# A transfer window of 1.5 MB, a seed product over 128 partitions, and the w_spatial sums on VectorE

## The chip, the core and the metric

The kernel runs on one core of a Trainium2 chip. The core has TensorE (PE; its weight loads are listed apart as PEld), VectorE (DVE), ScalarE (ACT), GpSimd (POOL), and SyncE (SP), which here issues nearly all transfers. Sixteen DMA engines move the data. The metric is the device time of one execution in microseconds. Everything is in 32-bit floats; a product on TensorE is made of three passes over operands that are split into a high part and a remainder (float32r).

## The reference

Chunked attention, then a gated MLP with a product over the positions. There are 4 batches, 8 heads of 64, 768 positions, chunks of 32 with 16 positions of context on the left and 8 on the right, and 8 memory positions.

```python
for c in range(nc):                      # 24 chunks of 32 positions
    k_full = concat([mem_k, k[l_start:r_end]]); v_full = concat([mem_v, v[l_start:r_end]])
    a = softmax(scale * q_c @ k_full.T)
    out[c] = a @ v_full
x = heads joined                         # (4, 768, 512)
h = maximum(x @ w_in, 0)                 # w_in (512, 1024)
u, v = h[..., :512], h[..., 512:]
v_n = (v - mean(v)) / sqrt(var(v) + 1e-6)
v_s = einsum('ts,bsd->btd', w_spatial, v_n) + b_spatial[None, :, None]
out = (u * v_s) @ w_out
```

w_in and w_out come as 64-bit floats and are turned into 32-bit ones on the chip.

## The kernel before

The kernel does not write its instructions in the order in which they run. Every piece of work is entered into a planner (`Plan`, lines 26 to 129) with its engine, an estimated duration, what it reads and writes, and a rank. `Plan.order` (64) simulates the engines and the transfers: at each step it takes, over all engines, the piece that can begin first, and among those of one engine the one with the lowest rank. `Plan.emit` (127) then issues all pieces in that order. The order on each engine, SP included, is thus fixed when the kernel is built. For transfers the planner assumes 0.30 MB per us for all of them together, 2 us for the landing, and that a transfer is not issued before the eighth transfer ahead of it has landed (lines 88 and 89). Loads that are entered with `seq=True` keep the order in which they are entered.

The work itself has two stages.

*Attention and first products.* 24 units of 128 positions (`attend`, 479): 64 small products for the scores of unit i and 64 for the weighted values of unit i - 1 (`burst`, 361, all on line 364), softmax on VectorE and ScalarE, transposes (448, 463). Behind each half of a batch come the products with w_in (`group`, 489, lines 501 to 503, 12 matmuls each). Their results are stored to DRAM: the normalized v by `ffn_v` (store on line 558, 256 KB) and u by `ffn_u` (store on line 575, 192 KB, from the ring `uo` of two buffers). The loads at the start are entered in this order (lines 921 to 936): the memory keys and values on ScalarE's queue; then on SP q and k of the first unit, two parts of w_in, v of unit 0 in four pieces, two parts of w_in, q and k of the second unit, v of unit 1, q and k of the next two units, v of unit 2, and the four parts of w_in for u.

*The products with w_spatial and w_out* (`product`, 609). Both are computed for each batch by a scheme of seven block products, p1 to p7, over quarters of the operands, in place of eight. Four sums of quarters, s1 to s4, are built on the left side: `total` (615, instruction on line 623) takes 128x768 elements at a time on the engine named by `sum_eng`, which is "POOL" in `spatial` (690, given on line 736) and "DVE" in `ffn_o` (739, given on line 782). `left` (627) splits each operand into a high part on ScalarE (636) and a remainder on VectorE (639). `blocks` (644) issues the matmuls (661). For w_spatial, the first product into a sum bank is preceded by a seed (655): a matmul of `ones` and `bias`, which adds b_spatial. Both have 64 partitions: row 0 holds the high part of the bias, row 32 its remainder, and all others are zero (`load_bias`, 893). There are 16 seeds, 4 in each batch. The results are copied from the banks (703, 752), joined (709, 758), and for w_spatial multiplied by u on POOL (717); for w_out they are stored (764). Of each batch, the first step for w_spatial is entered ahead of all steps for w_out of the batch before, and the other six behind them.

Of the kernel before, what the change touches and what calls it, by code (L numbers as in the profile page):

```python
# [9 lines left out]
F32R = mybir.dt.float32r  # L10
# [15 lines left out]
class Plan:  # L26
# [7 lines left out]

    def __init__(self, rings, loose, rate, landing, lat):
        self.rings, self.loose = rings, loose
        self.rate, self.landing, self.lat = rate, landing, lat
        self.ops, self.writer, self.readers, self.slots, self.newest = [], {}, {}, {}, {}
# [25 lines left out]
    def order(self):  # L64
# [17 lines left out]
        while len(out) < len(ops):  # L82
            best = None
            for e, ns in waiting.items():
                pick = None
                for n in ns:
                    t = max(free[e], ready[n], free["POOL"] if ops[n][9] else 0.0, lone if e == "POOL" else 0.0)
                    if ops[n][5] and len(landed) >= 8:
                        t = max(t, landed[-8])
                    for s in ops[n][7]:  # L90
                        have = taken[s[0]]
                        if s not in have and len(have) >= self.rings[s[0]]:
                            old = self.slots[have[-self.rings[s[0]]]]
                            t = max([t] + [end.get(m, 1e9) for m in old])
                    if t >= 1e9:
                        continue
                    late = max(t, free[e])
                    c = (late, ops[n][4], n)
                    if pick is None or c < pick:
                        pick = c  # L100
                if pick and (best is None or pick < best[0]):
                    best = (pick, e)
# [9 lines left out]
            if mb:  # L112
                pipe = max(pipe, t + us) + mb / self.rate
                end[n] = pipe + self.landing
                landed.append(end[n])
            else:
                end[n] = t + us + tail
            self.start[n] = t
            out.append((t, n))
            for m in users[n]:  # L120
                left[m] -= 1
                if not left[m]:
                    ready[m] = max([end[d] + self.lat for d in ops[m][3]] + [self.start[d] for d in ops[m][8]])
                    waiting[ops[m][0]].append(m)
        return [n for _, n in sorted(out)]

    def emit(self):
# [5 lines left out]
def tile_chunked_attention_gmlp(  # L133
# [45 lines left out]
             "q": 2, "k": 2, "kT": 2, "p": 1, "xs": 1, "pT": 1, "vr": 2, "op": 4, "sm": 2, "ug": 6, "ot": 8}  # L179
    plan = Plan(sizes, {"f", "y", "st", "big", "ot"}, rate=0.30, landing=2.0, lat=0.06)  # L180
    op = plan.op
# [20 lines left out]
    wsp = const.tile([P, 7, 2, HU, HT], F32R, name="wsp")  # L202
    bias = const.tile([D, 2, HT], F32R, name="bias")
    ones = const.tile([D, P], F32R, name="ones")
    ident = const.tile([P, P], F32, name="ident")
# [31 lines left out]
    line = {}  # L237

    def load(dst, src_, w, rank, r=(), eng="SP", slow=1.0, us=0.45, seq=False):
        e = {"SP": nc.sync, "ACT": nc.scalar, "POOL": nc.gpsimd}[eng]  # L240
        n = 4
        for s in src_.shape:
            n *= s
        mb = n / 1e6 * slow
        n = op(eng, us, lambda: e.dma_start(out=dst() if callable(dst) else dst, in_=src_), r=r, w=w, rank=rank, mb=mb,  # L245
               after=line.get(eng) if seq else None)
        if seq:
            line[eng] = n
# [273 lines left out]
    def ffn_v(b, tt):  # L522
# [26 lines left out]
        def norm():  # L549
# [7 lines left out]
        op("DVE", 0.43, norm, r=[("rstd", i)], w=[k_], rank=rank, alone=True)  # L557
        op("SP", 0.45, lambda: nc.sync.dma_start(out=vn_far[i // HU][:, i % HU], in_=t_["st", s]), r=[k_],
           w=[("vn_far", i // HU, i % HU)], rank=rank, mb=P * DH * 4e-6)

    def ffn_u(b, hf, d):
# [4 lines left out]
        def pair(c):  # L566
# [7 lines left out]
        far_ = u_far[(b * 2 + d // 2) * 2 + hf][:, d % 2]  # L574
        op("SP", 0.45, lambda: nc.sync.dma_start(out=far_, in_=t_["uo", i]), r=[("uo", i)],
           w=[("u_far", (b, d // 2, hf), d % 2)], rank=rank, mb=P * HT * 4e-6)
# [113 lines left out]
    def spatial(b):  # L690
# [4 lines left out]
        def done(name, p, bank):  # L695
# [37 lines left out]
            elif name == "p3":  # L733
                join("u2", bank)
                gate("u2", 0, 1)
        return product("s", b, ["p1", "p2", "p6", "p5", "p7", "p4", "p3"], [quarter(0, 0), quarter(0, 1), quarter(1, 0), quarter(1, 1)], HU, 2 * P, 2, HT,
                lambda i, x, s: wsp[:, i, x, s], lambda i: [("wsp", s, i) for s in range(HU)], "POOL", True, done)

    def ffn_o(b):
# [4 lines left out]
        def done(name, p, bank):  # L744
# [16 lines left out]
            def store(x, th, nh):  # L761
                r0 = (1 - th) * HT + p * P
                to = out[b, r0:r0 + P, nh * HN:(nh + 1) * HN]
                op("SP", 0.45, lambda: nc.sync.dma_start(out=to, in_=t_[ot(x)]), r=[ot(x)], rank=rank, mb=HN * P * 4e-6)
            if name == "p1":
# [127 lines left out]
    def load_bias(rank):  # L893
# [3 lines left out]
        def clear():  # L897
            t_[raw] = alloc("big", "bias", [P, 1024], U32).bitcast(F32)
            nc.gpsimd.memset(t_[raw][0:D], 0.0)
            nc.gpsimd.memset(t_[raw][0:D, S:S + P], 1.0)  # L900
        op("POOL", 0.8, clear, r=[("wsp", 2, 6)], w=[raw], rank=rank)
# [4 lines left out]
        def relative():  # L906
            a = t_[raw][0:D, HT:S]
            nc.gpsimd.tensor_tensor(a, a, t_[raw][0:D, 0:HT], op=ALU.subtract)

        def high():  # L910
            nc.scalar.copy(bias.rearrange("p h n -> p (h n)"), t_[raw][0:D, 0:S])
            nc.scalar.copy(ones, t_[raw][0:D, S:S + P])

# [111 lines left out]
```

## Time and profile before

| | us |
|---|---|
| median of 3 runs | 416.65 |
| range of the runs | 415.87 to 418.09 |
| the profiled execution | 417.55 |
| its span in the trace | 415.8 |
| busy in the span: PE, PEld | 375.4, 334.2 |
| busy in the span: DVE, ACT, POOL | 270.7, 192.8, 177.6 |
| mean granted TensorE clock | 0.979 |

The profile covers one execution. Matmuls overlap, so the distance between starts tells more than a duration. "PEclk" or the granted clock is the share of full speed that TensorE was given. The DMA share is the mean busy share of the 16 engines; it can be a little over 1, since packets overlap. In a timeline or a group, the bracket or the last column tells how long the engine had been idle and what ended that; "issue" is idle time in which the engine waited for nothing that the profile shows. "SPq" is the issuing of transfers by SP.

### The profile page before, as it was taken

How to read it: one execution, taken by the hardware profiler on the slowest of the kernel's cores; microseconds unless marked ns; L12 is line 12 of the kernel's file. 1: busy time of each engine (PE TensorE's matmuls, PEld its weight loads, DVE VectorE, ACT ScalarE, POOL GpSimd, SP SyncE). 2: the span in 40 equal slices, each digit the busy share in tenths (PEclk: the TensorE clock that was granted, in tenths of full speed). 3: DMA queues.
4: the chain of work that ended last, by engine and by line, in shares of the span. 5: the costliest groups of instructions: out<-in, count | busy, mean ns of one | idle time of the engine just before them, and what ended most of it. 6: DMA issues, size and time to landing. Idle time of an engine off the chain costs nothing.

```text
span 415.8 us, 11823 instructions
## 1 busy us (share of the span) xinstructions
PE 375.4 (90%) x4972; PEld 334.2 (80%) x4972; DVE 270.7 (65%) x446; ACT 192.8 (46%) x344; POOL 177.6 (43%) x167
## 2 busy tenths in 40 slices
PE   1576888799899799899999999999999999999985
PEld 0354667689798698788888899998999899989985
DVE  3656858385496596747686467668736883697373
ACT  3645426354554355434553347336434533552271
POOL 5322336553474095601131189443633364336510
PEclk9996689999999999999999999999999999999999
DMA  8999519828676766555732638306421542231004
GB/s 209 254 287 202 184 48 273 254 72 273 181 223 189 202 221 170 161 180 172 249 126 96 210 125 292 115 0 210 166 83 38 202 143 74 74 104 52 0 2 152
DMA packets 47369, 65.13 MB, mean 157 GB/s; under 512 B 4434, under 2 KB 38866, under 8 KB 47316
## 3 DMA queue, kind: packets, MB, share of 16 engines
q1 hardware_dynamic: 46900, 64.25, 51.0%
q8 instruction: 39, 0.64, 0.6%
q10 hardware_dynamic: 416, 0.13, 0.1%
q14 instruction: 14, 0.11, 0.1%
HBM read 45.49 MB, written 18.87 MB: 155 GB/s over the span
## 4 chain that ended last, share of the span: by engine, by line
PE 74%; DMA 10%; DVE 6%; issue 6%; ACT 2%; SPq 1%; ACTq 0%; DVEq 0%
PE y L661 17%; PE f L661 13%; PE f L501 11%; PE f L503 10%; PE f L502 10%; PE sx L364 8%; DMA vmain<-in_v_dram 6%; DVE op L639 3%; PE xt L463 2%; PE pt L448 2%; DMA k<-in_k_dram 2%; ACT op L636 1%; SPq L245 1%; DMA big<-in_moe_w_out_dram 1%; DVE ot L758 1%
## 5 line engine op out<-in xcount | busy, mean ns | idle before, releaser
L717 POOL TENSOR_TENSOR ug<-st,ug 128x384 f32<-128x384 f32 x32 | 41.6, 1310 | 30.5 <-DVE st L709 28.2
L661 PE MATMUL y<-wsp,op 128*128 128x384 f32 x288 | 54.0, 341 | 0.0
L661 PEld LDWEIGHTS y<-wsp,op 128*128 128x128 f32 x288 | 50.2, 188 | 1.5 <-issue 1.5
L501 PE MATMUL f<-x,win_h 128*128 128x384 f32 x128 | 46.2, 361 | 0.0
L636 ACT CAST op<-sm 128x768 fp32r<-128x768 f32 x32 | 26.7, 837 | 40.7 <-POOL sm L623 15.0
L639 DVE TENSOR_TENSOR op<-sm,op 128x768 fp32r<-128x768 f32 x32 | 34.2, 1068 | 15.9 <-ACT op L636 15.9
L503 PE MATMUL f<-x,win_h 128*128 128x384 f32 x128 | 43.2, 337 | 0.0
L501 PE MATMUL f<-win_h,x 128*128 128x512 f32 x96 | 43.1, 449 | 0.0
L502 PE MATMUL f<-x,win_l 128*128 128x384 f32 x128 | 43.0, 336 | 0.0
L547 POOL TENSOR_TENSOR rstd<-ve,mhalf 128x1 f32<-128x1 f32 x24 | 15.3, 638 | 64.3 <-DVE ve L543 64.0
L661 PE MATMUL f<-wsp,op 128*128 128x384 f32 x216 | 41.4, 342 | 0.0
L502 PE MATMUL f<-win_h,x 128*128 128x512 f32 x96 | 39.6, 413 | 1.3 <-issue 1.3
L503 PE MATMUL f<-win_l,x 128*128 128x512 f32 x96 | 39.6, 413 | 0.4 <-issue 0.4
L661 PEld LDWEIGHTS f<-wsp,op 128*128 128x128 f32 x216 | 37.4, 188 | 1.5 <-issue 1.1
L661 PE MATMUL y<-wout,op 128*128 128x256 f32 x288 | 36.3, 280 | 1.4 <-DVE op L639 0.9
L661 PEld LDWEIGHTS y<-wout,op 128*128 128x128 f32 x288 | 34.9, 188 | 2.0 <-DVE op L639 1.3
L400 DVE TENSOR_TENSOR xs<-sx,rec 128x512 f32<-128x512 f32 x24 | 16.5, 688 | 29.1 <-PE sx L364 29.1
L364 PE MATMUL sx<-vmain,pT 64*32 64x64 f32 x1536 | 24.5, 228 | 9.9 <-issue 8.9
L364 PEld LDWEIGHTS sx<-kmain,q 64*32 64x32 f32 x1536 | 17.9, 112 | 18.6 <-issue 10.1
L364 PE MATMUL sx<-kmain,q 64*32 64x64 f32 x1536 | 22.4, 238 | 10.7 <-ACT kmain L350 7.5
L364 PEld LDWEIGHTS sx<-vmain,pT 64*32 64x32 f32 x1536 | 20.2, 107 | 12.9 <-issue 11.0
L661 PE MATMUL f<-wout,op 128*128 128x256 f32 x216 | 28.1, 282 | 2.5 <-DVE st L758 2.3
(91 smaller groups left out, 766.0 us busy)
## 6 DMA issues: line engine op xcount, KB each, us to landing
vmain<-in_v_dram SPq DMA_DIRECT2D x48, 128.0 KB
vn_far<-st SPq DMA_DIRECT2D x24, 256.0 KB
u_far<-uo SPq DMA_DIRECT2D x32, 192.0 KB
vr<-vn_far SPq DMA_DIRECT2D x8, 768.0 KB
ug<-u_far SPq DMA_DIRECT2D x16, 384.0 KB
q<-in_q_dram SPq DMA_DIRECT2D x11, 512.0 KB
out_dram<-ot SPq DMA_DIRECT2D x36, 128.0 KB
vmain<-in_v_dram SPq DMA_DIRECT2D x47, 96.0 KB
```

The costliest lines, as they stand in the source:

```text
L364: nc.tensor.matmul(o, w_, m, start=True, stop=True, skip_group_check=True)
L400: nc.vector.tensor_tensor(xs.rearrange("p t r d -> p r t d"), t_["sx", i][:, :, 1], rec.rearrange("p t r -> p r t").unsqueeze(3).broadcast ...
L448: nc.tensor.transpose(a[:, t], p[:, t], ident)
L463: nc.tensor.transpose(a[:, t], xs[:, t], ident)
L501: nc.tensor.matmul(o, lh, rh, start=(j == 0), stop=False)
L502: nc.tensor.matmul(o, ll, rh, start=False, stop=False)
L503: nc.tensor.matmul(o, lh, rl, start=False, stop=(j == len(pairs) - 1))
L547: nc.gpsimd.tensor_tensor(a, t_["ve", i], mhalf, op=ALU.pow)
L636: nc.scalar.copy(half(0), of())
L639: nc.vector.tensor_tensor(half(1), of(), half(0).bitcast(F32), op=ALU.subtract)
L661: nc.tensor.matmul(o, x, y, start=first and m == 1 and not (seed and bank != "x"), stop=m == 3 * chunks, skip_group_check=True)
L717: nc.gpsimd.tensor_tensor(g, t_[st(x)], g, op=ALU.mult)
```

## The change

Three parts. A list `flight` takes down every transfer in the order of emission with its size in MB (the planner's own number: loads of q and k count 1.15 times, loads of v 1.2 times). Before a transfer is issued, `held_by` goes back through that list and adds up sizes, the new one included; the transfer at which the sum passes 1.5 MB, or else the eighth one back, must have landed first. The planner uses the same rule for its estimates, in place of the eighth one alone. Second, `bias` and `ones` have 128 partitions, and the clearing, the difference and the copies that make them cover 128 partitions; the added rows are zero in `bias`. Third, the four sums of `spatial` go to VectorE, in the planner (whose price for VectorE is 0.17 + 0.00102 us per element of a row, for POOL 0.15 + 0.0024) as in the code.

```diff
-    def __init__(self, rings, loose, rate, landing, lat):
+    def __init__(self, rings, loose, rate, landing, lat, window):
...
-                    if ops[n][5] and len(landed) >= 8:
-                        t = max(t, landed[-8])
+                    if ops[n][5]:
+                        t = max(t, self.held_by(landed, ops[n][5], 0))
...
-                landed.append(end[n])
+                landed.append((end[n], mb))
...
+    def held_by(self, flight, mb, none):
+
+        for back, (name, size) in enumerate(reversed(flight), 1):
+            mb += size
+            if back == 8 or mb > self.window:
+                return name
+        return none
...
-    plan = Plan(sizes, {"f", "y", "st", "big", "ot"}, rate=0.30, landing=2.0, lat=0.06)
+    plan = Plan(sizes, {"f", "y", "st", "big", "ot"}, rate=0.30, landing=2.0, lat=0.06, window=1.5)
...
-    bias = const.tile([D, 2, HT], F32R, name="bias")
-    ones = const.tile([D, P], F32R, name="ones")
+    bias = const.tile([P, 2, HT], F32R, name="bias")
+    ones = const.tile([P, P], F32R, name="ones")
...
+    flight = []
+
+    def transfer(e, out_, in_, mb):
+        ins = e.dma_start(out=out_, in_=in_)
+        wait = plan.held_by(flight, mb, None)
+        if wait:
+            tc.add_manual_dep(ins.ins, wait, mybir.DependencyInfo(mybir.DependencyClass.Sync, mybir.DependencyReason.DATA),
+                              reason="pace")
+        flight.append((ins.ins.name, mb))
...
-        n = op(eng, us, lambda: e.dma_start(out=dst() if callable(dst) else dst, in_=src_), r=r, w=w, rank=rank, mb=mb,
+        n = op(eng, us, lambda: transfer(e, dst() if callable(dst) else dst, src_, mb), r=r, w=w, rank=rank, mb=mb,
...
-                lambda i, x, s: wsp[:, i, x, s], lambda i: [("wsp", s, i) for s in range(HU)], "POOL", True, done)
+                lambda i, x, s: wsp[:, i, x, s], lambda i: [("wsp", s, i) for s in range(HU)], "DVE", True, done)
...
-            nc.gpsimd.memset(t_[raw][0:D], 0.0)
-            nc.gpsimd.memset(t_[raw][0:D, S:S + P], 1.0)
+            nc.gpsimd.memset(t_[raw][0:P], 0.0)
+            nc.gpsimd.memset(t_[raw][0:P, S:S + P], 1.0)
...
-            nc.scalar.copy(bias.rearrange("p h n -> p (h n)"), t_[raw][0:D, 0:S])
-            nc.scalar.copy(ones, t_[raw][0:D, S:S + P])
+            nc.scalar.copy(bias.rearrange("p h n -> p (h n)"), t_[raw][0:P, 0:S])
+            nc.scalar.copy(ones, t_[raw][0:P, S:S + P])
```

The stores on lines 558, 575 and 764 go through `transfer` in the same way, and the difference on line 908 covers 128 partitions.

More of the change, by code (lines that the diff above doesn't have):

```diff
@@ L26 @@
 class Plan:
-    def __init__(self, rings, loose, rate, landing, lat):
+    def __init__(self, rings, loose, rate, landing, lat, window):
         self.rings, self.loose = rings, loose
-        self.rate, self.landing, self.lat = rate, landing, lat
+        self.rate, self.landing, self.lat, self.window = rate, landing, lat, window
         self.ops, self.writer, self.readers, self.slots, self.newest = [], {}, {}, {}, {}
@@ L557, in ffn_v @@
         op("DVE", 0.43, norm, r=[("rstd", i)], w=[k_], rank=rank, alone=True)
-        op("SP", 0.45, lambda: nc.sync.dma_start(out=vn_far[i // HU][:, i % HU], in_=t_["st", s]), r=[k_],
+        op("SP", 0.45, lambda: transfer(nc.sync, vn_far[i // HU][:, i % HU], t_["st", s], P * DH * 4e-6), r=[k_],
            w=[("vn_far", i // HU, i % HU)], rank=rank, mb=P * DH * 4e-6)
@@ L574, in ffn_u @@
         far_ = u_far[(b * 2 + d // 2) * 2 + hf][:, d % 2]
-        op("SP", 0.45, lambda: nc.sync.dma_start(out=far_, in_=t_["uo", i]), r=[("uo", i)],
+        op("SP", 0.45, lambda: transfer(nc.sync, far_, t_["uo", i], P * HT * 4e-6), r=[("uo", i)],
            w=[("u_far", (b, d // 2, hf), d % 2)], rank=rank, mb=P * HT * 4e-6)
@@ L763, in store @@
                 to = out[b, r0:r0 + P, nh * HN:(nh + 1) * HN]
-                op("SP", 0.45, lambda: nc.sync.dma_start(out=to, in_=t_[ot(x)]), r=[ot(x)], rank=rank, mb=HN * P * 4e-6)
+                op("SP", 0.45, lambda: transfer(nc.sync, to, t_[ot(x)], HN * P * 4e-6), r=[ot(x)], rank=rank, mb=HN * P * 4e-6)
             if name == "p1":
@@ L906, in relative @@
         def relative():
-            a = t_[raw][0:D, HT:S]
-            nc.gpsimd.tensor_tensor(a, a, t_[raw][0:D, 0:HT], op=ALU.subtract)
+            a = t_[raw][0:P, HT:S]
+            nc.gpsimd.tensor_tensor(a, a, t_[raw][0:P, 0:HT], op=ALU.subtract)
         def high():
-            nc.scalar.copy(bias.rearrange("p h n -> p (h n)"), t_[raw][0:D, 0:S])
-            nc.scalar.copy(ones, t_[raw][0:D, S:S + P])
+            nc.scalar.copy(bias.rearrange("p h n -> p (h n)"), t_[raw][0:P, 0:S])
+            nc.scalar.copy(ones, t_[raw][0:P, S:S + P])
         def low():
```

## The prediction

> **What bounds the kernel now.** I read the page first (busy time and slices), then the table of stretches of 10 us, then the chain that ended last, and then the timelines of one batch. The page:
>
> ```profile
> span 415.8 us, 11823 instructions
> PE 375.4 (90%) x4972; PEld 334.2 (80%) x4972; DVE 270.7 (65%) x446; ACT 192.8 (46%) x344; POOL 177.6 (43%) x167
> DMA  8999519828676766555732638306421542231004
> ```
>
> TensorE is the bound, but not evenly. The stretches tell the stages apart (per engine: busy us and instructions; then granted clock, DMA share, GB/s):
>
> ```profile
> 30.00:40.00 10.00, 7.08 (x126) 5.20 (x126) 6.64 (x13) 5.21 (x10) 2.19 (x2) 0.66 1.05 231
> 40.00:50.00 10.00, 7.99 (x53) 6.09 (x61) 6.67 (x10) 4.22 (x9) 3.57 (x4) 0.66 0.55 158
> 50.00:60.00 10.00, 7.36 (x211) 5.71 (x209) 6.85 (x15) 3.83 (x8) 5.46 (x7) 0.83 0.29 94
> ...
> 290.00:300.00 10.00, 9.65 (x62) 9.22 (x62) 7.07 (x11) 3.05 (x6) 5.67 (x4) 1.00 0.40 138
> 300.00:310.00 10.00, 10.00 (x56) 9.56 (x56) 4.48 (x5) 4.00 (x7) 3.43 (x4) 1.00 0.38 137
> ```
>
> The first 40 us are bound by transfers (nine tenths and more in the slices, a share of 1.05 from 30 to 40 us), with TensorE busy 7 of 10 us and its clock cut to 0.66 from 30 to 50 us. From about 250 us, where the w_spatial and w_out products run, TensorE is busy all of 300 to 310 us and misses 0.35 us in the stretch before. What is saved there must come out of TensorE's own stream.
>
> **Part one: bias and ones on 128 partitions.** The seed product of each sum bank (L655) now contracts 128 rows, 64 of them zero, instead of 64. Its neighbours (L661) contract 128. The rows of its shape, and the TensorE timeline around two of the 16 (8 into y, 8 into f):
>
> ```profile
> L661 PEld LDWEIGHTS y<-wsp,op 128*128 128x128 f32 x288 | 50.2, 188 | 1.5 <-issue 1.5
> L655 PE MATMUL y<-bias,ones 64*128 64x384 f32 x8 | 3.5, 437 | 0.0
> L655 PEld LDWEIGHTS y<-bias,ones 64*128 64x128 f32 x8 | 1.5, 183 | 2.0 <-issue 2.0
> 299.60 0.44 PE L655 MATMUL f<-bias,ones 64*128 64x384 f32 x1
> ...
> 301.75 0.44 PE L655 MATMUL f<-bias,ones 64*128 64x384 f32 x1
> 302.12 1.85 PE L661 MATMUL f<-wsp,op 128*128 128x384 f32 x9
> 303.81 6.52 PE L661 MATMUL y<-wsp,op 128*128 128x384 f32 x36
> 310.17 3.35 PE L661 MATMUL f<-wsp,op 128*128 128x384 f32 x18
> ```
>
> Starts, not durations, count, since matmuls overlap. 36 products take 310.17 - 303.81 = 6.36 us, 0.177 us each. A seed with its nine takes 301.75 - 299.60 = 2.15 us, where ten at 0.177 would take 1.77: the 64-row one costs 0.38 us more than a 128-row one, before and after it. The weight-load rows show why it isn't the work itself: 183 ns against 188, but with 2.0 us of idle before 8 of them. 16 x 0.38 = **6.1 us**, all in the stage where TensorE has nothing else to wait for. The ends: 0 if the added cost stays with a seed of 128 rows, 6.1 if it becomes like its neighbours; I take 6.1, since the 9 that follow have that very shape and pay 0.177.
>
> A rule speaks against this term. The Trainium skill, TensorE: Matmul & The Clock Gate, LDWEIGHTS (loading the stationary operand), says that a weight load takes as long for 32 rows as for 128; the rows agree (183 and 188 ns), and by it alone the term would be 0 (a rival below). Against it stands TensorEngine Tiling (Array Packing), Key Properties, in the same skill: a change of tiling mode drains the engine; the idle before the loads agrees with this one.
>
> The rest of this part: two clears, one difference and two copies on twice the partitions with the same length per partition. They run once, near 160 us on POOL and ScalarE; TensorE reads the result from 248 us on, so nothing waits. If it did, they are 0.9 + 1.0 + 0.8 us by the rows of their present form: no end of the range.
>
> **Part two: the sums for the w_spatial product.** 16 sums of 128x768 (four per batch) go from POOL to VectorE.
>
> ```profile
> L623 DVE TENSOR_TENSOR sm<-ug 128x768 f32<-128x768 f32 x8 | 7.6, 953 | 0.1
> 282.44 1.85 POOL L623 TENSOR_TENSOR sm<-vr 128x768 f32<-128x768 f32 x1 [6.91 <-DVE op L639]
> 282.86 3.11 DVE L639 TENSOR_TENSOR op<-ug,op 128x768 fp32r<-128x768 f32 x2 [0.50 <-ACT op L636]
> 285.89 0.94 DVE L639 TENSOR_TENSOR op<-sm,op 128x768 fp32r<-128x768 f32 x1
> 286.98 1.84 POOL L623 TENSOR_TENSOR sm<-sm,vr 128x768 f32<-128x768 f32 x1 [2.70 <-DVE op L639]
> 287.43 2.20 DVE L639 TENSOR_TENSOR op<-vr,op 128x768 fp32r<-128x768 f32 x1
> 290.35 3.07 PE L661 MATMUL f<-wout,op 128*128 128x256 f32 x24 [0.74 <-DVE st L758]
> L661 PE MATMUL f<-wout,op 128*128 128x256 f32 x216 | 28.1, 282 | 2.5 <-DVE st L758 2.3
> ```
>
> VectorE takes on 16 x 0.95 = 15.2 us. It gets some of that back: the same split takes 0.94 us alone (285.89) and 2.20 while a POOL sum runs (287.43), 1.26 more; the pair at 282.86 takes 3.11 where two alone take 1.88, 1.23 more. Two such overlaps per batch and four batches are about 10 us, so VectorE gains some 5 us of work over 160 us, and it has room: 4.48 of 10 us busy in 300 to 310.
>
> On the path is one place per batch: the split at 287.43 ends late, the joins at L758 behind it end late, and TensorE idles 0.74 us before 290.35; the group's row gives 2.3 us of that over all batches. With the sum placed right ahead of that split on VectorE, both take 0.95 + 0.94 = 1.89 instead of 2.20: 0.3 us less, in three batches (the last has no next batch's sum there) **0.9 us**. Ends: 2.3 us gained if the sum moves elsewhere; 4 x 0.95 = 3.8 us lost if each batch gets one sum ahead of a join that TensorE awaits. I take 0.9 gained, nearest to the rows. POOL's gates (L717) behind the sums come earlier or stay; they aren't what TensorE waits for in the fences above.
>
> **Part three: the window.** Each transfer now waits, on its queue, for the older ones that would take the sum over 1.5 MB (the planner's own sizes: loads of q and k count 1.15 times, of v 1.2 times), or for the eighth older one. From SP's timeline, the transfers' sizes, the chain (start, length) and the queues:
>
> ```profile
> 2.79 2.90 SPq L245 DMA_DIRECT2D vmain<-in_v_dram  x4
> 11.87 2.25 SPq L245 DMA_DIRECT2D vmain<-in_v_dram  x4
> vmain<-in_v_dram SPq DMA_DIRECT2D x48, 128.0 KB
> vmain<-in_v_dram SPq DMA_DIRECT2D x47, 96.0 KB
> big<-in_moe_w_in_dram SPq DMA_DIRECT2D x8, 512.0 KB
> q<-in_q_dram SPq DMA_DIRECT2D x2, 256.0 KB
> k<-in_k_dram SPq DMA_DIRECT2D x1, 256.0 KB
> 2.79 9.06 DMA vmain<-in_v_dram
> 29.10 2.45 issue
> 39.40 2.58 issue
> 50.98 2.65 issue
> 409.92 1.64 DMA out_dram<-st
> q8 instruction: 39, 0.64, 0.6%
> ```
>
> A limit by count exists: the transfer issued at 2.79 landed at 11.85, and SP issued again at 11.87. In between stand, in the code's order of loads, eight transfers: four pieces of v (448 KB), two parts of w_in, and the second halves of the first q and k: 2.03 MB, or 2.20 as the planner counts. So the window binds in the first 40 us and takes about a third out of what is under way. Loads are issued in a fixed order, so as long as something is under way, the same bytes land in the same order at the same rate, and the later issue costs nothing: the cover is the transfer still running. Behind a waiting load on SP stand other loads, later also the stores of u and v.
>
> Does the cover hold? The store on the chain, with little ahead of it, landed 1.64 us after its issue began; no released transfer needs more until its first data. One 512 KB part left under way lasts 0.52 MB / 231 GB/s = 2.3 us. It holds, by 0.6 us. Some 16 transfers of 256 KB or more go out in the first 33 us (8 of w_in, the rest q and k); if a quarter of them found only a 128 KB piece under way (0.6 us), that is 4 x 1.0 = 4 us lost. The other end: 39 blocks of 0.64 MB / 39 = 16 KB of instructions come through the same engines, one per 255 of the 2 x 4972 instructions of TensorE, and TensorE stops for 2.45 and 2.58 us in "issue" in the middle of bursts while transfers are dense. With 0.6 MB less ahead of it, a block would come up to 2.6 us sooner: up to 5.0 us gained. Against that, the third stop (50.98) is as long where the DMA share is 0.29. So between 4 lost and 5 gained I take **1.0 gained**: the data's part is covered, and of the two stops a fifth is counted.
>
> The window and the new prices also change the written order of all engines' work; which burst meets a block's end shifts with it. I know no row for that and leave it in the ends above.
>
> **Sum.** The profiled execution took 417.55 us (span 415.8 and 1.75 around it). 417.55 - 6.1 - 0.9 - 1.0 = 409.55. The median of the runs shown, 416.65, lies 0.9 below that execution, so 408.65 in its terms; all times below are in these terms.
>
> **Rivals.**
> *The blocks come in time and the clock stays up.* Both stops go (5.0 us), and so does the cut clock: a granted 0.66 over 20 us loses 6.8 us of clock, at three quarters busy 5 us of work, of which data waits keep back an estimated half. 416.65 - 7.0 - 5.0 - 2.5 = 402.2. For it: the clock falls right after the stops. Against: the third stop.
> *The saved time turns into waits on VectorE.* Each batch's 1.5 us is given back at the joins; the window's 1.0 remains: 415.7. For it: VectorE is busy 7.07 in 290 to 300 us. Against: 4.48 in the next ten.
> *The seed keeps its price*, which is then that of a change of operands and not of rows: 416.65 - 1.9 = 414.75. For it: the two kinds of weight load take the same time. Against: the nine behind it change operands too, at 0.177.
> *The window does nothing on the path.* The change then doesn't do what it says: 416.65 - 7.0 = 409.65. For it: after 40 us the DMA share is mostly below 0.8. The Trainium skill, Runtime: NRT & Kernel Launch, Instruction fetch mechanics, has the crossing of a block mostly hidden, which would give this time; the three stops disagree with it.
> *Slower: the window holds up SP.* Place: the pairs of q and k loads of the attention, by their shapes 0.60 + 0.64 MB as the planner counts; the next store of the normalized v (256 KB, 0.26) passes 1.5 and stops SP until q has landed, and the store of u behind it keeps one of two buffers of ScalarE's output, so that TensorE's bank stays full. It decides once such a store lands later than two groups of 12 products take (2 x 12 x 0.177 = 4.2 us). At an estimated 1 us on TensorE for each of 11 such pairs, and the window's gain gone: 416.65 - 7.0 + 11 = 420.7. Against: the row below, where ScalarE has lost only 1.7 us to these stores.
>
> ```profile
> L572 ACT ACTIVATE uo<-f 128x384 f32<-128x384 f32 x32 | 15.6, 491 | 15.9 <-PE f L503 14.0 <-DMA u_far<-uo 1.7
> ```
>
> **How the numbers follow.** Forecast 0.50 (its own range 404 to 413), clock 0.11, VectorE 0.11, seed 0.05, idle window 0.12, SP 0.11. Changes under 0.5% (2.1 us) can't be told from none here; 414.57 and 418.73 are the bounds. Faster: 0.48 + 0.11 + 0.01 + 0.02 + 0.12 = 0.74, with the seed's case near the bound; same: 0.02 + 0.10 + 0.03 = 0.15; slower 0.11. The range 402 to 418 leaves out the SP case and about half of the clock case, 0.17.
>
> **What would show it.** Part one: L655 as 128*128, its start and the next 0.177 us apart. Part two: splits near 0.95 us, no L623 on POOL, the 0.74 us wait before L758's products shorter. Part three: vmain landings of 6 to 7 us instead of 9.06, at the same GB/s in the first 40 us. It would be wrong if TensorE showed new idle time after 250 us, if the GB/s of the first stretches fell, or if "issue" grew.

## The result, and the profile after

| | before, us | after, us |
|---|---|---|
| median (4 runs each) | 417.37 | 403.98 |
| range | 415.87 to 418.23 | 400.97 to 404.88 |
| the profiled execution, its span | 417.55, 415.8 | 404.88, 403.0 |

The ratio is 0.967, with a 95% interval of 0.961 to 0.973. Medians and ranges are over all executions; ratios with their intervals, and medians marked "fast", leave out executions more than 1.5% above the fastest of the same kernel. The changed kernel is faster by 13.4 us; the forecast was 408.7 with a range of 402 to 418. The direction and the range held, but the gain was two thirds larger than the 8.0 us of the sum, and its three terms were all too small.

The page of the kernel after (busy time in us, share of the span, instructions; then the DMA slices):

```profile
span 403.0 us, 11801 instructions
PE 365.8 (91%) x4972; PEld 334.4 (83%) x4972; DVE 272.7 (68%) x462; ACT 190.7 (47%) x344; POOL 151.8 (38%) x151
DMA  7987767835693877646582443832640544041004
```

TensorE is still the bound. VectorE has taken on 16 instructions and yet is only 2.0 us busier than before (272.7 against 270.7): the 16 sums that it took on cost it 17.1 us by their rows, and other instructions of it became shorter. POOL lost 26 us. The stretches of 10 us of the kernel after (per engine busy us and instructions; granted clock, DMA share, GB/s):

```profile
30.00:40.00 10.00, 7.31 (x90) 5.41 (x89) 6.77 (x14) 6.23 (x12) 3.21 (x4) 0.83 0.78 212
40.00:50.00 10.00, 5.68 (x203) 4.54 (x203) 9.01 (x16) 5.43 (x10) 6.11 (x7) 0.83 0.68 196
50.00:60.00 10.00, 8.57 (x160) 6.95 (x161) 7.78 (x16) 3.64 (x7) 4.92 (x5) 0.83 0.69 179
290.00:300.00 10.00, 10.00 (x59) 10.00 (x59) 6.46 (x9) 3.97 (x7) 3.35 (x2) 1.00 0.35 112
300.00:310.00 10.00, 10.00 (x60) 10.00 (x59) 5.70 (x8) 3.33 (x6) 7.40 (x6) 1.00 0.20 74
```

The DMA engines are no longer full throughout the first 40 us, and from 290 us TensorE and its weight loads miss nothing. The clock is cut less deep from 30 to 50 us, but its mean is 0.979 in both profiles, so this brought no net gain here; the later cuts come back below.

To tell the stages apart I use one cut in the text that follows: the start of TensorE's matmul no. 3828 (counted from 0) of 4972, some 22 us ahead of the first product with w_spatial. It lies at 226.0 us before and 225.0 after; from there to the start of the last matmul it is 185.2 us before and 173.9 after. This length hardly differs between executions: the kernel after took 173.9 to 174.0 in each of three profiles. So 11.3 us of the gain lie in the second stage. In the new written order another product carries this number than in the old one; that this doesn't shift the comparison is seen below, where the window alone has the length of before and the first two parts alone that of after. The first stage of the kernel after took 220.4 to 225.0 us in the same three profiles, and what the window gives must be read there.

The TensorE timeline of the kernel after around two seeds, and its groups that answer to those of before (the columns are as there):

```profile
294.69 0.34 PE L673 MATMUL f<-bias,ones 128*128 128x384 f32 x1
...
296.43 0.34 PE L673 MATMUL f<-bias,ones 128*128 128x384 f32 x1
...
298.17 6.40 PE L679 MATMUL y<-wsp,op 128*128 128x384 f32 x36
304.41 3.29 PE L679 MATMUL f<-wsp,op 128*128 128x384 f32 x18
```

```profile
L673 PEld LDWEIGHTS y<-bias,ones 128*128 128x128 f32 x8 | 1.5, 188 | 0.0
L657 DVE TENSOR_TENSOR op<-vr,op 128x768 fp32r<-128x768 f32 x12 | 11.4, 954 | 12.9 <-ACT op L654 12.9
L679 PE MATMUL f<-wout,op 128*128 128x256 f32 x216 | 27.0, 279 | 0.0
```

A seed with its nine now takes 296.43 - 294.69 = 1.74 us (2.15 before), the idle time before the seeds' loads is gone (2.0 before), and 36 other products take 304.41 - 298.17 = 6.24 us (6.36 before). The split that took 1482 ns on average takes 954. The 2.3 us for which TensorE had waited behind the joins are 0.0.

The chain of the kernel after (start, length, what), its long stops in "issue" in the middle of work:

```profile
28.30 3.82 issue
...
73.58 2.19 issue
107.35 2.44 issue
...
169.30 1.34 issue
```

Counted in TensorE's own stream (matmuls, weight loads and the few waits between them), work goes on behind these four with instructions 705, 2241, 3521 and 5825, that is with 193 + 256 x 2, 8, 13 and 22: they stand at the ends of blocks of 256 instructions. Here they sum to 9.8 us. Before, six such stops sum to 12.1, three of them at the same places (2, 13 and 22). Whether this difference is more than chance is a question for the experiments.

### The profile page after: what moved, and what is told of

It is laid out like the page before. It is cut to its first block, busy times and chain, and to the rows that moved or that the text cites. A ratio compares the mean times of both kernels' runs of the same rounds, so it can differ in the third digit from the quotient of the medians.

```text
span 403.0 us, 11801 instructions
## 1 busy us (share of the span) xinstructions
PE 365.8 (91%) x4972; PEld 334.4 (83%) x4972; DVE 272.7 (68%) x462; ACT 190.7 (47%) x344; POOL 151.8 (38%) x151
## 4 chain that ended last, share of the span: by engine, by line
PE 73%; DMA 9%; DVE 7%; issue 5%; ACT 3%; SPq 0%; ACTq 0%; DVEq 0%
PE y L679 20%; PE f L679 15%; PE f L519 9%; PE f L520 8%; PE f L521 8%; PE sx L382 7%; DMA k<-in_k_dram 3%; PE xt L481 3%; PE pt L466 2%; DMA big<-in_moe_w_in_dram 1%; PE f L534 1%; DMA big<-in_moe_w_out_dram 1%; DVE st L569 1%; DMA q<-in_q_dram 1%; DMA big<-in_moe_w_spatial_dram 1%
## 5 line engine op out<-in xcount | busy, mean ns | idle before, releaser
L735 POOL TENSOR_TENSOR ug<-st,ug 128x384 f32<-128x384 f32 x32 | 43.2, 1363 | 87.0 <-DVE st L727 67.7
L679 PE MATMUL y<-wsp,op 128*128 128x384 f32 x288 | 52.6, 336 | 0.0
L679 PE MATMUL f<-wsp,op 128*128 128x384 f32 x216 | 40.1, 336 | 0.0
L657 DVE TENSOR_TENSOR op<-sm,op 128x768 fp32r<-128x768 f32 x32 | 31.8, 997 | 11.6 <-ACT op L654 11.5
L654 ACT CAST op<-sm 128x768 fp32r<-128x768 f32 x32 | 26.4, 838 | 26.3 <-DVE sm L641 14.4
L382 PEld LDWEIGHTS sx<-kmain,q 64*32 64x32 f32 x1536 | 18.0, 112 | 20.5 <-issue 13.4
L382 PEld LDWEIGHTS sx<-vmain,pT 64*32 64x32 f32 x1536 | 20.1, 108 | 11.2 <-issue 6.7
L721 ACT COPY st<-y 128x384 f32<-128x384 f32 x32 | 15.4, 480 | 28.0 <-PE y L679 27.7
```

The source lines that it names most:

```text
L382: nc.tensor.matmul(o, w_, m, start=True, stop=True, skip_group_check=True)
L654: nc.scalar.copy(half(0), of())
L657: nc.vector.tensor_tensor(half(1), of(), half(0).bitcast(F32), op=ALU.subtract)
L679: nc.tensor.matmul(o, x, y, start=first and m == 1 and not (seed and bank != "x"), stop=m == 3 * chunks, skip_group_check=True)
L721: op("ACT", act(HT), lambda: nc.scalar.copy(alloc("st", st(x)[1], [P, HT], F32), t_[bank]), r=[bank], w=[st(x)], rank=rank)
L735: nc.gpsimd.tensor_tensor(g, t_[st(x)], g, op=ALU.mult)
```

## The experiments

### Each part alone

Three kernels that each hold one part. For the first, of the change above only the lines of the tiles `bias` and `ones` and of what fills them:

```diff
-    bias = const.tile([D, 2, HT], F32R, name="bias")
-    ones = const.tile([D, P], F32R, name="ones")
+    bias = const.tile([P, 2, HT], F32R, name="bias")
+    ones = const.tile([P, P], F32R, name="ones")
...
```

> Part one alone (128-partition seed; the order of every engine is that of the kernel before). Theory 'seed': the trace of after has every start in the w_spatial stage 0.1735 us apart, where before had 0.174 and 0.179 in turn behind each seed; so this part alone brings the 16 x 0.38 = 6.1 us of the prediction and some 1.2 us more from the stream behind the seeds: 410 us against 417.4, and the idle before the joins' products (2.3 us in all) stays. Rival 'only the seed': 6.1 us, 411.3, and the starts go on alternating between 0.174 and 0.179. Rival 'the seed keeps its price': 417.4.

For the second, only the engine of the sums of `spatial`:

```diff
-                lambda i, x, s: wsp[:, i, x, s], lambda i: [("wsp", s, i) for s in range(HU)], "POOL", True, done)
+                lambda i, x, s: wsp[:, i, x, s], lambda i: [("wsp", s, i) for s in range(HU)], "DVE", True, done)
```

> Part two alone (the four sums of each batch on VectorE; TensorE's order is that of the kernel before, the seeds have 64 rows). Theory 'joins': before lost 1.3 us of starts per batch around the joins behind the slowed split, three times, and some at the end; all of it goes: 4 us, 413.4 us, with no idle before the w_out products of a batch. Rival, the prediction's term: 0.9 us, 416.5. Rival 'VectorE becomes late': 3.8 us slower.

For the third, the window in the planner and in the transfers, with the tiles and the engine as before:

```diff
+    plan = Plan(sizes, {"f", "y", "st", "big", "ot"}, rate=0.30, landing=2.0, lat=0.06, window=1.5)
...
+        wait = plan.held_by(flight, mb, None)
```

> Part three alone (real waits and the planner's rule; the order of all engines changes). Theory 'small': 1 to 2 us in the first 240 us, 415.5 to 416.4. Rival 'large': the window brings what parts one and two do not, 5 to 6 us, 411.5 to 412.5, with less issue idle and more clock in the first 60 us. In both, TensorE's time from 240 us on is as before.

| | median, us (range) | second stage, us | gain there |
|---|---|---|---|
| before, same chip | 415.96 (406.45 to 419.45) | 185.2 | |
| bias and ones alone | 408.72 (405.33 to 412.20) | 178.0 | 7.2 |
| sums alone | 411.19 (409.26 to 415.20) | 181.1 | 4.2 |
| window alone | 413.79 (411.93 to 416.23) | 185.3 | 0.0 |

The gains of the first two parts in the second stage add up: 7.2 + 4.2 = 11.4 us, against 11.3 in the kernel with all three. The window moves nothing there; what it has, some 2 us by the medians, must lie in the first stage. On this chip the kernel before scattered over 13 us, so the medians only give the order of size; the second stage is the sharp number.

For the sums alone, the groups and the timeline of TensorE at the joins:

```profile
L639 DVE TENSOR_TENSOR op<-vr,op 128x768 fp32r<-128x768 f32 x12 | 12.3, 1023 | 14.3 <-ACT op L636 14.2
L661 PE MATMUL f<-wout,op 128*128 128x256 f32 x216 | 27.0, 279 | 0.0
```

```profile
290.25 3.66 PE L661 MATMUL f<-wout,op 128*128 128x256 f32 x30
```

The 30 matmuls run through, where before the last 24 of them began after an idle 0.74 us. Start by start, before loses 3.4 us among the products of the f bank, at one stretch of joins in each of the first three batches, 0.7 where the products of the y bank pass to those of f just ahead of them, and 2.2 among those of y at the end of the last batch. With the sums on VectorE the 2.2 alone remain: 3.4 + 0.7 = 4.1 of the 4.2. The sums themselves now stand behind the split, between the joins (at 290.09 and 291.49 us, the split at 288.52).

### Is it the two engines side by side?

If POOL's sums hurt only because they were late, VectorE's own sums would cure it whatever POOL does. The changed kernel was therefore given each of the 16 sums once more, on POOL, into a tile that nothing reads; this is extra work and the output does not depend on it.

```diff
-            ps["y"] = pool("ps_y", bufs=sizes["y"], space=PSUM, side="right")
+            ps["y"] = pool("ps_y", bufs=sizes["y"], space=PSUM, side="right"); t_["spare"] = pool("spare", bufs=1, side="right").tile([P, S], F32, name="spare")
...
-            op(sum_eng, dve(W) if sum_eng == "DVE" else pool_(W), go, r=keys, w=[sm], rank=rank)
+            op(sum_eng, dve(W) if sum_eng == "DVE" else pool_(W), go, r=keys, w=[sm], rank=rank); seed and op("POOL", pool_(W), lambda: nc.gpsimd.tensor_tensor(t_["spare"].rearrange("p (s n) -> p s n", s=chunks), in0(), in1(), op=o), r=keys, w=["spare"], rank=rank)
```

> The changed kernel with each of the 16 sums computed once more on POOL, into a spare buffer that nothing reads; TensorE's order is the same. Theory 'a POOL sum beside a split makes VectorE late': splits of about 2.2 us come back, and TensorE loses 4 us or more after 225 us: 408 or more. Rival 'the sum itself came too late on POOL' (1.84 us and its place in the queue): nothing waits for the spare sums, so 404 as before.

Beside it ran the changed kernel itself:

> The changed kernel again, beside the next three on one chip: 402 to 405 us by any theory. It is the base for the other three.

The changed kernel took 400.86 us (ratio 0.965, 0.960 to 0.970; 402 to 405 had been expected), the one with POOL's extra sums 416.24 (1.004, 1.000 to 1.008): the whole gain of the change is lost to work that no instruction waits for in the trace. The second stage is 186.4 us, 12.5 more. That is three times what moving the sums had won, since VectorE makes its own sums here too; and a few instructions of VectorE (22 of 462 places) and of ScalarE (6 of 344) also changed their order, while TensorE's order is the same. The run thus shows the mechanism, not the price that the sums had before. Its timeline:

```profile
287.77 2.85 PE L679 MATMUL f<-wout,op 128*128 128x256 f32 x23
...
288.59 1.84 POOL L642 TENSOR_TENSOR spare<-sm,vr 128x768 f32<-128x768 f32 x1 [13.26 <-DVE sm L641]
288.90 2.35 DVE L641 TENSOR_TENSOR sm<-sm,vr 128x768 f32<-128x768 f32 x1
291.17 0.41 DVE L776 TENSOR_TENSOR ot<-f,ot 128x256 f32<-128x256 f32 x1
...
291.63 0.97 PE L679 MATMUL f<-wout,op 128*128 128x256 f32 x6 [1.01 <-DVE ot L776]
...
295.10 1.85 POOL L642 TENSOR_TENSOR spare<-vr,sm 128x768 f32<-128x768 f32 x1 [2.16 <-DVE sm L641]
295.35 2.42 DVE L657 TENSOR_TENSOR op<-sm,op 128x768 fp32r<-128x768 f32 x1
```

A VectorE instruction that begins 0.31 us after POOL's takes 2.35 us where it takes 0.95 alone; it ends at 291.25, which is 0.82 after POOL's end at 290.43. The other begins 0.25 us after and ends 0.82 after POOL's end too. So it stands nearly still until POOL is done and then takes nearly its own time. The same holds for all of them: 12 sums and splits of VectorE begin while one of POOL's extra sums runs, and each ends 0.81 to 0.89 us after it; in the kernel before it is 10 of 11, with 0.81 to 0.89 us too. The Trainium skill, SBUF — State Buffer, SBUF: two separate sides, calls this an exclusive lock on a port pair, held for the whole instruction by the one that starts first; these rows agree. The joins (L776), which read one operand from the sum bank, keep their time: the 9 that begin while such a sum runs take 0.40 to 0.41 us. The wait of TensorE behind a join (1.01 us) is back, as before the change.

### The window: the order, the waits, or the first loads?

The window does two things: it changes what the planner assumes, hence the written order, and it makes transfers wait. The changed kernel with the planner's window and no real waits:

```diff
-        wait = plan.held_by(flight, mb, None)
+        wait = None
```

> The changed kernel without the waits of the window: the order of every engine is that of the changed kernel, but transfers are held back only by what they were held by before. If the order that the planner makes with the window brings its gain, this stays at 404.0 us. If the real waits bring it (less under way, blocks of instructions sooner), this is 1 to 5 us slower than the changed kernel, with longer stops in issue in the first 60 us.

> The changed kernel's order without the real waits, beside it on one chip. Theory 'order': within 1 us of the changed kernel, since the loads keep their order and TensorE's products from 225 us on are the same. Rival 'blocks of instructions come sooner with less under way': 1 to 5 us slower than the changed kernel, all of it before 225 us.

The changed kernel with neither (the first two parts in the old order):

> Parts one and two with the order that the planner makes without the window. If the parts add up, the window's part is what this lacks: 1 to 3 us slower than the changed kernel, all before 225 us, and from there to the end the same 173.9 us. If they don't, this is 404 (the window is worth nothing beside the other two).

On the first chip the order without waits took 405.32 us (400.68 to 406.33), with nothing of the complete kernel beside it. On the second chip it took 408.60 (402.92 to 410.32; fast 405.29), the first two parts without a window 404.00 (397.01 to 406.73; fast 401.87), the complete change 400.86 (396.65 to 405.03; fast 400.22). So the new order by itself brings nothing: by these medians it loses 4.6 us (fast 3.4), the waits within it win 7.7 (fast 5.1), and the window as a whole is worth 3.1 (fast 1.7). The ranges overlap, and three such differences of medians are not proof. (The order's second profile, with a granted clock of 0.964, and that of the two parts without a window are left out of the first stages below.)

What the waits do at the start can be seen in ScalarE's timeline, first of the kernel before, then of the kernel after:

```profile
8.41 0.67 ACT L796 ACTIVATE st<-big 128x512 f32<-128x512 f32 x1 [1.40 <-DMA big<-in_moe_w_in_dram]
...
11.11 0.66 ACT L796 ACTIVATE st<-big 128x512 f32<-128x512 f32 x1 [1.47 <-DMA big<-in_moe_w_in_dram]
```

```profile
7.25 0.67 ACT L814 ACTIVATE st<-big 128x512 f32<-128x512 f32 x1 [0.61 <-DMA big<-in_moe_w_in_dram]
...
9.31 0.67 ACT L814 ACTIVATE st<-big 128x512 f32<-128x512 f32 x1 [0.82 <-DMA big<-in_moe_w_in_dram]
```

The first two parts of w_in are taken 1.2 and 1.8 us sooner, although SP issues the second one later, at 4.21 in place of 2.31 us. And the total rate of the first 35 us is 228 GB/s in place of 246. Transfers that are under way thus share the engines, and holding back the later ones lets the earlier ones land. Is this the gain? Three more kernels ask, together with the changed one. The first keeps the waits for the first 12 transfers alone:

```diff
-        wait = plan.held_by(flight, mb, None)
+        wait = plan.held_by(flight, mb, None) if len(flight) < 12 else None
```

> The changed kernel with the waits kept for the first 12 transfers alone (the first q and k, four parts of w_in, four pieces of v, the second q and k); every later transfer is issued without a wait for older ones. All engines' order is unchanged. Theory S (sharing at the start): transfers under way share the DMA engines, and the window gains by letting the first parts of w_in land before the rest is started; then nearly all of its gain is here: ScalarE takes the second part of w_in at 9.3 to 10.6 us, as with all waits (11.1 to 12.4 without), and the time is that of the changed kernel on this chip within 1.5 us. Theory L (sharing all along): each later load is served earlier as well; then the second part still comes at 9.3 to 10.6 us but the first stage is longer and the time lies 2 to 4 us above the changed kernel's, near that of the order alone. Theory N: the window's 3 us were noise between executions; then it makes no difference here which waits are kept, and all four kernels of this call agree within 1.5 us.

The two others leave the written order alone and set another real limit, 1.0 and 2.0 MB:

```diff
-    def held_by(self, flight, mb, none):
+    def held_by(self, flight, mb, none, limit=1.5):
...
-            if back == 8 or mb > self.window:
+            if back == 8 or mb > limit:
...
-        wait = plan.held_by(flight, mb, None)
+        wait = plan.held_by(flight, mb, None, 1.0)
```

> The changed kernel, its written order planned with 1.5 MB as before, but its transfers really wait until no more than 1.0 MB is under way. Theories S and L: the earliest loads have the engines to themselves still more, so the second part of w_in is taken no later than at 9.3 us and the first exp by 9.9 us; but the total rate in the first 35 us falls further, from 228 to 233 GB/s to about 215, and with some 8 MB to be moved there that costs 2 us or more: 1 to 4 us slower than the changed kernel. The prediction's own reading (same bytes in the same order at the same rate, cover of 2.3 us against 1.64): with 1.0 MB a 512 KB part still covers a start, so no change. Theory N: no change within 1.5 us.

> The changed kernel, its written order planned with 1.5 MB, but its transfers really wait until no more than 2.0 MB is under way. Theories S and L: between the changed kernel and the order alone: the second part of w_in is taken between 10 and 12 us, the rate in the first 35 us lies at 235 to 245 GB/s, and the time is 0 to 3 us above the changed kernel's. Theory N: no difference within 1.5 us, and no trend over 1.0, 1.5 and 2.0 MB.

> The changed kernel itself once more, beside the three others on the same chip: 398 to 405 us, ratio to the kernel before 0.96 to 0.97; the second part of w_in taken by ScalarE at 9.3 to 9.7 us; rate in the first 35 us 228 to 233 GB/s; time from TensorE's matmul 3828 to its last 173.9 us. It is the base from which the other three are read.

| real waits | median, us (range) | first stage | second part of w_in taken at | stops at block ends |
|---|---|---|---|---|
| 1.5 MB (the change) | 402.09 (397.83 to 404.54) | 221.2 | 10.0 | 8.2 |
| 1.5 MB, first 12 transfers | 405.62 (400.16 to 408.63) | 226.0 | 10.1 | 11.2 |
| 2.0 MB | 403.13 (398.67 to 407.03) | 218.7 | 11.2 | 7.3 |
| 1.0 MB | 433.97 (432.60 to 435.46) | 255.6 | 12.4 | 3.6 |

The rows behind the fourth column, ScalarE's timeline for waits on the first 12, and for 2.0 MB:

```profile
10.10 0.67 ACT L814 ACTIVATE st<-big 128x512 f32<-128x512 f32 x1 [1.23 <-DMA big<-in_moe_w_in_dram]
```

```profile
11.16 0.67 ACT L814 ACTIVATE st<-big 128x512 f32<-128x512 f32 x1 [1.14 <-DMA big<-in_moe_w_in_dram]
```

By the medians alone this isn't settled. The 12 waits lie 3.5 us above the change (fast 2.2), where a gain at the start alone asked for at most 1.5, and loads served earlier all along for 2 to 4; 2.0 MB lies 1.0 above it (fast 0.9 below), and up to 3 above was allowed by both. But in one profile of each, with waits on the first 12 transfers the part comes early and the first stage is as long as before; with 2.0 MB it comes late and the first stage is the shortest.

And the written order is the same, so the starts can be compared matmul by matmul: at matmul 346, just ahead of TensorE's stop at 29 us, the 12 waits are 0.4 and 2.0 MB 0.2 us behind the change. The early landing is worth no more than that by then. In the first profile after, the reason can be seen: TensorE next stands for 2.54 us until k of the second unit, which the window holds back, has come (ScalarE waits 2.23 us for it), and goes on at 19.99 us, against 20.30 before.

What goes with the first stage is the last column. The chains (start, length, what) of the changed kernel in this series, of the one with 12 waits, of 2.0 MB, and of the order without waits:

```profile
28.89 4.34 issue
...
72.67 1.92 issue
104.69 1.12 issue
...
163.80 0.86 issue
```

```profile
29.28 4.65 issue
...
73.31 3.01 issue
107.88 1.98 issue
...
169.64 1.60 issue
```

```profile
29.13 4.16 issue
...
73.04 0.90 issue
103.93 0.92 issue
...
162.67 1.32 issue
```

```profile
28.37 4.98 issue
...
73.62 2.58 issue
106.26 2.25 issue
...
168.22 1.32 issue
```

All four stop at the same four instructions. What TensorE waits for there is the next block: in all 14 profiles, work goes on 1.2 to 1.6 us after the end of a packet of the instruction queue, at every stop over 0.6 us at a block's end. With waits for all transfers the sum is 9.8, 8.2, 8.0, 8.2 and 7.3 us (the first profile after, the window alone, the second and the third profile of the change, 2.0 MB); without them, or with the first 12, it is 11.1, 12.0 and 11.2. No value of the one lies among the other; the means are 8.3 and 11.5. In the old order without waits it is 11.6 to 15.1 (four profiles). (The kernel with POOL's extra sums, which has all waits, fits in with 8.9 us and a first stage of 222.3.) The first stages go along, though their ranges overlap: 218.7 to 225.0, mean 221.4, with all waits, 224.5 and 226.0 without. So 3.2 us of stops (2.9 without the order's second profile) stand against 3.8 us of time (221.4 against the mean of the two, 225.2).

The starts show that the time is lost there. Each block end taken with the few microseconds behind it, the 12 waits lose 0.3, 2.7, 2.4 and 0.7 us against the change at these four places, 6.1 in all, of which 4.8 are left at the end of the first stage. The order without waits, in its first profile, loses 3.3 of its 4.1 us there against the second profile of the change (on another chip). Only half of the 6.1 us are the stops themselves (11.2 - 8.2 = 3.0). Most of the other half is the clock: the rows of the 12 waits (clock, DMA share and GB/s in the last three columns) have 0.86 and 0.83 behind the second and the third stop, where the change beside them has 1.00 in both. In the trace it is half the clock for 3.4 us each time, from 77.3 and from 111.4 us.

```profile
70.00:80.00 10.00, 6.99 (x149) 5.77 (x149) 3.50 (x6) 2.90 (x5) 5.68 (x5) 0.86 0.95 285
...
110.00:120.00 10.00, 10.00 (x146) 8.16 (x144) 7.02 (x15) 3.92 (x7) 6.24 (x7) 0.83 0.55 166
```

The first profile of the change has such cuts behind the same two stops, from 76.4 and 110.5 us, and the longest first stage of the three, 225.0.

Why are the stops shorter with the waits? Worked out from the packets of the instruction queue in the trace, the mean time over the first 24 blocks from TensorE's entry into a block to the start of the next fetch is 2.1 to 2.4 us in the old order without waits, 1.8 to 2.0 in the new one without all waits, and 1.7 to 1.8 with them. A block's packet itself takes about 1.1 us in all of them. This speaks for a fetch that has to find its turn among the data. It isn't proved: it is one profile for most of these kernels, and between 1.5 and 2.0 MB the stops don't grow with what may be under way. One row speaks against it: in the kernel before, the fetch behind the block that TensorE enters at 42.0 us starts only at 51.2, although the DMA share from 40 to 50 us is 0.55. How the engines give out the turns, no run here shows.

The rates of the first 35 us of the change and of 1.0 MB (the last three columns: clock, DMA share, GB/s):

```profile
0.00:35.00 35.00, 15.36 (x353) 10.85 (x354) 17.30 (x33) 15.73 (x26) 12.30 (x17) 0.96 0.87 227
```

```profile
0.00:35.00 35.00, 14.57 (x333) 10.70 (x336) 16.84 (x30) 13.96 (x23) 11.73 (x17) 1.00 0.64 169
```

The limit of 1.0 MB went far beyond what any theory had put down (1 to 4 us, or no change): 31.9 us slower than the change. It leaves a third of the engines idle, 169 GB/s in place of 227, and even the second part of w_in comes later: two parts together pass 1.0 MB, so it isn't issued until the first has landed, at 8.05 us in place of 4.50. What SP's queue waited for (us in total, times, longest), at 1.0 MB and then in the changed kernel:

```profile
SPq L250 <- DMA q<-in_q_dram: 40.2, 12, 4.2
SPq L250 <- DMA k<-in_k_dram: 32.9, 11, 3.6
```

```profile
SPq L250 <- DMA q<-in_q_dram: 15.1, 11, 3.1
...
SPq L250 <- DMA k<-in_k_dram: 5.8, 4, 1.7
```

SP stands 52 us longer behind landings of q and k. Of the 73 us, 35.6 are loads of k that wait for q of their own pair, since the two together pass 1.0 MB. With such a load under way little else may start, and after a landing there is little under way until the next data come. That its stops at block ends are few proves little, as its first stage is 34 us longer, and a block can come in the pauses.

Between 1.5 and 2.0 MB there is no difference that these runs can tell. No kernel here was faster than the change. On this third chip its own ratio to the kernel before was 0.983 (0.970 to 0.996), where 0.96 to 0.97 had been expected: the kernel before itself ran from 405.95 to 418.47 there, and the ratio goes by the lowest two of its eleven executions. By the medians of all it is 0.973, and the second stage took the expected 174.0 us.

## Why the prediction was right, and where not

**Part one, 6.1 us: 7.2.** Mechanism right, a part of the size left out. The seed's own price was met: from bias and ones alone to the kernel before, the start of a seed is 0.269 us behind the one ahead of it in place of 0.177, the next start 0.367 in place of 0.174, and the next 0.278 in place of 0.175. That is 0.39 us, 6.2 for 16, where the prediction had 0.38 and 6.1. The step "ten at 0.177" took the pace of the neighbours for the pace without a seed, and this pace was slowed itself: behind 14 of the 16 seeds of 64 rows the starts alternate between 174 and 179 ns, up to the products with w_out; with 128 rows nearly all are 173 or 174. This is the other 1.1 us. That the weight loads take the same time held (183 ns with 64 rows, 188 with 128); that the term would then be 0 did not, as the idle time before them is gone. The rival that the seed keeps its price fell with it. Which part of TensorE keeps the altered rhythm isn't shown.

**Part two, 0.9 us: 4.2.** The mechanism and the three places were right; each place was worth 1.4 us and not 0.3. The step that failed is the sum placed "right ahead of that split" with "both take 0.95 + 0.94 = 1.89 instead of 2.20". The sums did not stand in the way: VectorE does them behind the split, between joins, 0.95 us each, and TensorE is not waiting there. So the split and the pair ahead of it are rid of both delays by POOL, 1.26 and 1.23 us, with nothing put in their place, and the wait went not by 0.3 us of 0.74 but entirely. The upper end, 2.3 us, came from the idle column of one group's row, that of f; start by start f lost 3.4, and 0.7 more went where y's products pass to f's. That range was thus too small, and the rival of waits on VectorE had no ground.

**Part three, 1.0 us: about 3, for one of its two reasons.** "The same bytes land in the same order at the same rate, and the later issue costs nothing" failed: the rate fell by 7% (246 to 228 GB/s in 35 us), and bytes that were issued first landed sooner. The sign put down for it, that a fall in GB/s would show the forecast wrong, was a bad sign: the time fell all the same, as the stage doesn't end with the last byte. The landing of v after 9.06 us is no longer on the chain, so the sign of 6 to 7 us can't be read there. The early landing was not the gain either, as the starts at matmul 346 show. The other reason is the one that the runs bear out: the stops for blocks of instructions are shorter when transfers wait, and so are the stretches of cut clock behind them. Why a block then comes sooner isn't shown. It was counted at a fifth of 5.0 us because of the third stop in a quiet stretch; by the sums of stops it is worth 3.2 us or a little less, though one first profile on each side (12.1 and 9.8) wouldn't have shown it to be more than chance. "Issue" did not vanish, and the mean granted clock stayed at 0.979, so the rival of 402.2, whose time came nearest, was not what happened: it wanted the stops gone and the clock up, where TensorE's second stage gave the difference. It was right in that the clock falls behind several of the longer stops. The Trainium skill, Runtime: NRT & Kernel Launch, Instruction fetch mechanics, has these crossings mostly hidden; with 7 to 15 us of stops in one execution of every kernel but that of 1.0 MB, these traces do not agree.

**The other rivals.** The idle window is made unlikely by the two series and not more: by the medians beside the change (404.00 and 405.62 against 400.86 and 402.09) the window, or its later waits, is worth 3.1 and 3.5 us (fast 1.7 and 2.2), near their scatter. SP held up by the window came at 1.5 MB where it had been placed, but small: in the first profile after, SP waits 7.8 us in all for q ahead of stores of v and u, ScalarE loses 3.4 us to the stores of u in place of 1.7, and TensorE 1.2 us, once; in the third profile it is 8.4, 3.7 and 0. At 1.0 MB such stores wait 14.6 us, and the loads of k behind q cost more.

That the result was covered owes something to luck: 403.98 lies just below the forecast's own range (404 to 413), and inside 402 to 418 only because the lower end was drawn for the rival of the blocks and the clock. All three terms were too small.

7.2 + 4.2 + 3 = 14.4 us, against 13.4 measured first and 14.5 on the second chip (415.34 to 400.86). On the third it was 11.3 (413.34 to 402.09).

## What to carry to other kernels

Where TensorE runs without a break, read the starts of a whole stretch and not of one instruction: a small matmul of another shape slows what follows it as well, and the pace of its neighbours is not the clean pace. A large two-operand instruction on POOL is paid for by VectorE, so a sum that POOL does "for free" can cost more than doing it on VectorE. A limit on the transfers under way can shorten stops at the ends of instruction blocks, but it has a steep side: at 1.5 and 2.0 MB it won some 3 us by the medians, at 1.0 MB it lost 32 against that, so the limit wants a margin; here a pair of q and k loads counts 1.24 MB.

## What was not expected of the hardware

- 64 rows among 128 cost more than the instruction: 0.4 us at the seed, and mostly a stream of 174 and 179 ns in turn behind it where nearly all are 173 or 174 otherwise.
- TensorE stopped for 0.7 to 5.2 us at ends of blocks of 256 instructions, in dense work, until 1.2 to 1.6 us after a packet of the instruction queue, and less long when all transfers kept to a limit of 1.5 or 2.0 MB (8.3 us in sum on average, 11.5 without, in one written order). Behind some of the longer stops it ran for 3.4 us at half the clock.
- With later transfers held back, an earlier one landed 1 to 2 us sooner at a total rate 7% lower.
- A VectorE instruction with two operands in SBUF, begun 0.3 us behind one of POOL, ended 0.82 us after POOL's, at 2.35 us in place of 0.95; all 12 that met such a sum ended 0.81 to 0.89 us after it.
